# GpSimd takes over the high-word scaling of the weight conversions and half of the early softmax normalisation

## The chip, the cores and the metric

The kernel runs on one core of a Trainium2 chip. The metric is the device time of one execution in microseconds. TensorE (PE), VectorE (DVE), ScalarE (ACT) and GpSimd (POOL) each work through their own queue of instructions in order; SyncE (SP) issues the DMA transfers.

## The reference

A causal attention over a window of 128 positions, with a linear bias by distance for each of 8 heads, feeds two MLPs. Cut to what matters:

```python
scores = (q @ k.T) / 8 + bias          # 4 batches, 8 heads, 576 positions, head size 64
scores = where(0 <= i - j < 128, scores, -1e9)
attn = exp(scores - max);  attn = attn / (sum(attn) + 1e-9)
x = (attn @ v)                         # as 2304 tokens x 512
x = (s * relu(x @ w_in1)**2 + b) @ w_out1     # 512 -> 2048 -> 512
out = relu(x @ w_in2)**2 @ w_out2             # the same shape
```

All inputs and the output are float32. The four weight matrices reach the chip as 64-bit words: the host hands in float64 copies, viewed as integers.

## The kernel before, in words

**Weights.** Each weight matrix comes in four groups of 512 rows or columns of the hidden size. A load on SP's queue fills a tile `st...` of 128 partitions with 1024 or 512 pairs of 32-bit words (the low word and the high word of a float64). `convert` turns such a tile into float32 and splits it into a rounded part (`wih`, `woh`) and the rest (`wil`, `wol`), so that products of rounded parts in three passes stand for a float32 product. Its chain of seven steps goes from engine to engine: L123 on ACT (low word), L124 on DVE (sign), L125 (high word times 2^-112, in place; this is the line of the change), L126 on DVE (a shift, in place), L127 on POOL (integer add of the two words), L99 on ACT (rounded copy), L105 on DVE (the rest). Words of a kind lie 8 bytes apart in the tile. There are 14 conversions of 1024 words a partition and 4 of 512 for the first MLP, which all lie in the first 160 us, and 32 of 512 for the second, which lie between 508 and 658 us.

**Attention.** `pair_unit` handles 256 (or 128 + 256) query rows of two heads. Its first half makes scores on PE (L249), adds the bias tile `bases` on DVE (L190), takes exponentials on ACT (L194) and reciprocals of the sums on DVE (L197, L198). Its second half divides (L270 for the first head of the units of batch 0, L272 for all else), transposes the probabilities on PE (L274), copies the transposes out of PSUM on ACT (L99), multiplies with v on PE (L285) and splits the result into `x0h`, `x0l` (ACT, then DVE L102). In the names, `f_0_2woh` is the probability tile of batch 0's row block 0, units 2 and 3, `nd_0_3` the sums of unit 3, `t_0_3` its transposes, `u_0_3` its output. The eight units of batch 0 (u = 0 and 1, four pairs of heads) are the early ones. They come first in the program, together with the conversions of group 0 (`st_211`, `st_265`, `st_315`, `st_326`) and the first of group 1 (`st_337`, `st_480`).

**MLPs.** `mlp` runs over the hidden size in steps of 128: L361 (first product, 12 matmuls), ACT L371, DVE L372, ACT L99, DVE L105, then L398 or L407 (second product). Attention units and conversions are interleaved as pieces "behind" these steps, and a scheduler then sets each engine's order.

**Bias tiles.** The eight `bases` (L79) are made on POOL before anything else there, one for each head:

```python
nc.gpsimd.tensor_scalar(bases[:, h, :], base, 8.0 * 2.0 ** (-8.0 * (h + 1) / H), None, ALU.mult)
```

Of the kernel before, what the change touches and what calls it, by code (L numbers as in the profile page):

```python
# [8 lines left out]
F32 = mybir.dt.float32  # L9
# [3 lines left out]
AF = mybir.ActivationFunctionType  # L13
ALU = mybir.AluOpType
# [5 lines left out]
def attention_mlp2_kernel(ctx, tc, first0, first1, qkv0, qkv1, qkvt, w_in1, w_out1, s_in, b_in, w_in2, w_out2, out):  # L20
# [7 lines left out]
    nc = tc.nc  # L28
    B, H = qkv0.shape[:2]
# [31 lines left out]
    base = ap.tile([P, 2 * W], F32, tag="pr", name="base", bufs=NPR)  # L61
# [14 lines left out]

    bases = ap.tile([P, H, 2 * W], mybir.dt.bfloat16, tag="bases", name="bases", bufs=1)
    for h in range(H):
        nc.gpsimd.tensor_scalar(bases[:, h, :], base, 8.0 * 2.0 ** (-8.0 * (h + 1) / H), None, ALU.mult)  # L79

    tqs = [ap.tile([P, 2, TAIL], F32, tag=f"tq{i}", name=f"tq{i}", bufs=1) for i in range(2)]
    for t in tqs:
# [8 lines left out]
    def split(hi, lo, src, copy, sub):  # L91
        copy(hi, src)
        sub(lo, src, hi.bitcast(F32))
# [4 lines left out]
    def act_copy(o, i):  # L98
        return nc.scalar.activation(o, i, AF.Copy)  # L99
# [13 lines left out]
    def convert(words, hi, lo):  # L113

        l32, h32 = words[..., 0], words[..., 1]
        with tc.issue_after(marks[-4]) if len(marks) > 3 else nullcontext():
            nc.scalar.activation(l32, l32.bitcast(U32), AF.Copy, scale=2.0 ** -29)  # L123
        nc.vector.scalar_tensor_tensor(l32, h32, -2 ** 31, l32, ALU.bitwise_and, ALU.bitwise_or)  # L124
        nc.scalar.activation(h32.bitcast(F32), h32.bitcast(F32), AF.Copy, scale=2.0 ** -112)  # L125
        nc.vector.tensor_scalar(h32, h32, 3, None, ALU.logical_shift_left)  # L126
        nc.gpsimd.tensor_tensor(l32, h32, l32, ALU.add)  # L127
        split(hi, lo, l32.bitcast(F32), act_copy, dve_sub)
# [5 lines left out]
    def group_loads(g, wts, w_in, w_out, staging, steps):  # L134
# [22 lines left out]
        def conv(i):  # L157
            _, k, n, step = parts[i]
            if k not in wts[g]:
                for j in (k, k + 1):  # L160
                    wts[g][j] = wp.tile([P, GF, DM], F32R, tag=f"{GTAGS[j]}{g}", name=f"{GTAGS[j]}{g}")
            hi, lo = wts[g][k], wts[g][k + 1]
            part = (slice(None), slice(n, n + step)) if k else (slice(None), slice(None), slice(n * P, (n + step) * P))
            convert(places.pop(i).rearrange("p a (n w) -> p a n w", w=2), hi[part], lo[part])
# [37 lines left out]
    def pair_unit(b, u, hp):  # L202
# [56 lines left out]
        def outputs():  # L259
            raw, den, probs, pts = (made[x] for x in ("raw", "den", "probs", "pts"))  # L260
            vr = raw[:, BLK + nj * P:n].rearrange("p (j a d) -> p j a d" if early else "p (a j d) -> p j a d", j=nj, d=D)
            for i, (_, ncol) in enumerate(tiles):
                tp = (psum("h", f"t{nm}").rearrange("p (i n) -> p i n", n=P) if early and not (i or u) else
                      ps.tile([P, 4, P], F32, tag="t", name=f"t{nm}{i}", bufs=1))
                m = 0
                for a in range(2):
                    pr = probs[a][:, i, :ncol]
                    rden = den[:, 2 * a + i:2 * a + i + 1]
                    if early and a == 0:
                        nc.scalar.activation(pr, pr, AF.Copy, scale=rden)  # L270
                    else:
                        nc.vector.tensor_scalar(pr, pr, rden, None, ALU.mult)  # L272
                    for j in range(ncol // P):
                        nc.tensor.transpose(tp[:, m, :], pr[:, j * P:(j + 1) * P], ident)  # L274
                        m += 1
                moved = act_copy(pts[i][:, :m, :], tp[:, :m, :])
            up = ps.tile([P, 3 * P], F32, tag="u", name=f"u{nm}", bufs=1) if hp % 2 or u or not early else psum("o", f"u{nm}")

            with tc.issue_after(moved.ins):
                k = 0  # L280
                for i, (ka, ncol) in enumerate(tiles):
                    nk = ncol // P
                    for j in range(nk):
                        for a in range(2):
                            nc.tensor.matmul(up[a * D:(a + 1) * D, i * P:(i + 1) * P], vr[:, ka // P + j, a, :],  # L285
                                             pts[i][:, a * nk + j, :], start=(k == 0), stop=(j == nk - 1),
                                             skip_group_check=True)
                        k += 1
            xh, xl = xt[(b, u)]
            split(xh[:, hp, :], xl[:, hp, :], up[:, :BLK], act_copy if early and u else act_mark, dve_mark)  # L290
# [153 lines left out]
    def psum(tag, name):  # L444
        return pools["ps"].tile([P, DM], F32, tag=tag, name=name)
# [184 lines left out]
```

## Time and profile before

| what | value |
|---|---|
| time, median of 3 runs | 999.97 us (999.9 to 1000.04) |
| span of the profiled execution, first to last instruction | 996.9 us |
| left between that span and the median | 3.1 us |
| busy: PE, DVE, ACT, POOL | 968.4, 519.4, 489.5, 80.6 us |
| mean granted TensorE clock | 0.983 of full speed |

The page gives the profiled execution's span and no other time of it; 3.1 us of the median lie around it. Busy time is an average over stages: the first 160 us (attention of batch 0 and the conversions of the first MLP) look unlike the rest, so they are read by themselves.

### The profile page before, as it was taken

The page shows a single profiled execution, that of the slowest core. Times are in us where ns is not written, and L with a number is a line of the kernel's source. Part 1 is how long each engine was busy: PE and PEld are TensorE (multiplying, and loading weights), DVE is VectorE, ACT ScalarE, POOL GpSimd, SP SyncE. Part 2 cuts the span into 40 slices and gives each one's busy share as a digit, 9 for nine tenths or more (in the row PEclk, how much of TensorE's full clock was granted, in tenths as well). Part 3 has the DMA queues.
Part 4 walks back from the last instruction along what each step waited for, and adds up shares of the span by engine and source line. Part 5 has one row for each costly group of instructions (what it writes and reads, how often), then busy time and mean ns, then how long its engine had stood idle before and what let it go on. Part 6 is the DMA issues. An engine that isn't in the chain of part 4 may idle for free.

```text
span 996.9 us, 16799 instructions
## 1 busy us (share of the span) xinstructions
PE 968.4 (97%) x6504; PEld 852.6 (86%) x6504; DVE 519.4 (52%) x1268; ACT 489.5 (49%) x1157; POOL 80.6 (8%) x86
## 2 busy tenths in 40 slices
PE   7999899999999999999999999999999999999997
PEld 4699689999999999999999888778888888898886
DVE  6986886344764647646266787744222322422222
ACT  7976766455565545644255677654222321322121
POOL 4320320000000000000011222210000000000000
PEclk9699989999999999999999999999999999999999
DMA  8144423111221212211052445422000100100001
GB/s 337 44 157 152 149 94 107 54 54 34 67 65 42 78 29 74 75 46 29 27 178 85 131 170 155 137 75 84 1 1 22 43 1 1 43 1 22 1 1 42
DMA packets 46927, 72.39 MB, mean 73 GB/s; under 512 B 6656, under 2 KB 27136, under 8 KB 46848
## 3 DMA queue, kind: packets, MB, share of 16 engines
q1 hardware_dynamic: 46848, 71.32, 22.0%
q8 instruction: 51, 0.84, 0.4%
q14 instruction: 28, 0.23, 0.1%
HBM read 59.77 MB, written 11.53 MB: 72 GB/s over the span
## 4 chain that ended last, share of the span: by engine, by line
PE 77%; DMA 8%; ACT 6%; DVE 6%; issue 2%; POOL 0%; SPq 0%; ACTq 0%; DVEq 0%; POOLq 0%
PE ob L407 15%; PE hb L361 14%; PE ha L361 14%; PE oa L398 13%; DMA st<-w_out 4%; PE oc L398 3%; PE s L249 3%; PE u L285 3%; PE hc L361 3%; DMA st<-w_in 3%; PE t L274 2%; PE hbtail L361 2%; PE obtail L407 2%; DMA xib<-acc 1%; DVE wil L105 1%
## 5 line engine op out<-in xcount | busy, mean ns | idle before, releaser
L398 PE MATMUL oa<-ga,woh 128*128 128x256 f32 x960 | 188.7, 288 | 4.4 <-DVE ga L105 2.3
L407 PE MATMUL ob<-woh,gb 128*128 128x512 f32 x512 | 168.7, 390 | 1.2 <-ACT gb L99 1.2
L398 PEld LDWEIGHTS oa<-ga,woh 128*128 128x128 f32 x960 | 151.6, 191 | 9.0 <-DVE ga L105 3.1
L398 PE MATMUL oa<-ga,wol 128*128 128x256 f32 x480 | 135.9, 286 | 0.0
L372 DVE SCALAR_TENSOR_TENSOR rb<-hb,rb 128x512 f32<-128x512 f32 x64 | 44.1, 690 | 147.4 <-ACT rb L371 147.2
L407 PEld LDWEIGHTS ob<-woh,gb 128*128 128x128 f32 x512 | 96.0, 188 | 23.1 <-ACT gb L99 3.2
L371 ACT ACTIVATE rb<-hb 128x512 f32<-128x512 f32 x64 | 38.2, 596 | 156.3 <-PE hb L361 152.0
L407 PE MATMUL ob<-wol,gb 128*128 128x512 f32 x256 | 99.7, 389 | 0.0
L398 PEld LDWEIGHTS oa<-ga,wol 128*128 128x128 f32 x480 | 91.7, 191 | 1.3 <-issue 0.9
L127 POOL TENSOR_TENSOR st<-st 128x512 int32<-128x512 int32 (+1 forms) x50 | 68.9, 1379 | 285.1 <-DVE st L126 285.1
L372 DVE SCALAR_TENSOR_TENSOR ra<-ha,ra 128x256 f32<-128x256 f32 x120 | 50.1, 418 | 49.0 <-ACT ra L371 48.1
L105 DVE TENSOR_TENSOR ga<-ra,ga 128x256 fp32r<-128x256 f32 x120 | 57.1, 478 | 26.6 <-ACT ga L99 25.9
L105 DVE TENSOR_TENSOR gb<-rb,gb 128x512 fp32r<-128x512 f32 x64 | 45.5, 710 | 44.0 <-ACT gb L99 43.9
L99 ACT ACTIVATE ga<-ra 128x256 fp32r<-128x256 f32 x120 | 49.2, 413 | 38.0 <-DVE ra L372 36.0
L371 ACT ACTIVATE ra<-ha 128x256 f32<-128x256 f32 x120 | 45.1, 377 | 42.6 <-PE ha L361 41.3
L99 ACT ACTIVATE gb<-rb 128x512 fp32r<-128x512 f32 x64 | 40.4, 631 | 47.6 <-DVE rb L372 35.6
L124 DVE SCALAR_TENSOR_TENSOR st<-st 128x512 int32<-128x512 int32 (+1 forms) x50 | 46.7, 937 | 25.1 <-ACT st L123 24.7
L123 ACT ACTIVATE st<-st 128x512 int32<-128x512 uint32 (+1 forms) x50 | 40.9, 822 | 33.0 <-DMA st<-w_out 19.9
L407 PEld LDWEIGHTS ob<-wol,gb 128*128 128x128 f32 x256 | 48.1, 188 | 9.8
L194 ACT ACTIVATE pr<-pr,nd 128x256 f32<-128x256 f32 (+1 forms) x96 | 45.1, 472 | 6.3 <-DVE nd L190 6.3
L190 DVE CUSTOM_DVE_ANT_0 pr<-s,bases 128x256 f32<-128x256 f32 (+1 forms) x96 | 31.9, 386 | 23.7 <-PE t L274 14.6
L125 ACT ACTIVATE st<-st 128x512 f32<-128x512 f32 (+1 forms) x50 | 40.7, 818 | 5.7 <-DVE st L124 5.7
(204 smaller groups left out, 2348.6 us busy)
## 6 DMA issues: line engine op xcount, KB each, us to landing
st<-w_out SPq DMA_DIRECT2D x20, 512.0 KB, 3.9
st<-w_in SPq DMA_DIRECT2D x8, 1024.0 KB, 6.0
st<-w_in SPq DMA_DIRECT2D x16, 512.0 KB, 4.5
st<-w_out SPq DMA_DIRECT2D x6, 1024.0 KB, 9.8
raw<-qkv SPq DMA_DIRECT2D x36, 128.0 KB, 2.6
xib<-acc SPq DMA_DIRECT2D x9, 512.0 KB, 4.6
out<-obb SPq DMA_DIRECT2D x16, 256.0 KB, 2.0
raw<-qkv SPq DMA_DIRECT2D x24, 160.0 KB, 3.0
```

What stands on the lines that cost most here:

```text
L99: return nc.scalar.activation(o, i, AF.Copy)
L105: nc.vector.tensor_tensor(o, a, b_, ALU.subtract)
L123: nc.scalar.activation(l32, l32.bitcast(U32), AF.Copy, scale=2.0 ** -29)
L124: nc.vector.scalar_tensor_tensor(l32, h32, -2 ** 31, l32, ALU.bitwise_and, ALU.bitwise_or)
L125: nc.scalar.activation(h32.bitcast(F32), h32.bitcast(F32), AF.Copy, scale=2.0 ** -112)
L127: nc.gpsimd.tensor_tensor(l32, h32, l32, ALU.add)
L194: nc.scalar.activation(pr, pr, AF.Exp, bias=nmx, scale=-1.0, accum_out=den)
L361: nc.tensor.matmul(ph, w_[:, cc, j * P:(j + 1) * P], x_[:, cc, :], start=(k == 0), stop=(k == 3 * NCC - 1))
L371: nc.scalar.activation(r, ph, AF.Relu)
L372: nc.vector.scalar_tensor_tensor(r, ph, 0.0, r, ALU.max, ALU.mult)
L398: nc.tensor.matmul(po[o // 2][:, (o % 2) * BLK:(o % 2 + 1) * BLK], w_[:, j, o * P:(o + 1) * P], g[:, gi, :], start=(start and n == 0 and o ...
L407: nc.tensor.matmul(po[t], g[:, gi, t * P:(t + 1) * P], w_[:, j, :], start=(start and n == 0), stop=(stop and n == 2))
```

## The change

Three operations are written for POOL as a tensor_scalar with two multiplications, the second by 1.0. L79 was on POOL already, with one multiplication. L125 (50 instructions: 14 on 1024 words, 36 on 512) and L270 (16 instructions: 12 on 128x256, 4 on 128x128) were on ACT.

```diff
     for h in range(H):
-        nc.gpsimd.tensor_scalar(bases[:, h, :], base, 8.0 * 2.0 ** (-8.0 * (h + 1) / H), None, ALU.mult)
+        nc.gpsimd.tensor_scalar(bases[:, h, :], base, 8.0 * 2.0 ** (-8.0 * (h + 1) / H), 1.0, ALU.mult, ALU.mult)
...
         nc.vector.scalar_tensor_tensor(l32, h32, -2 ** 31, l32, ALU.bitwise_and, ALU.bitwise_or)
-        nc.scalar.activation(h32.bitcast(F32), h32.bitcast(F32), AF.Copy, scale=2.0 ** -112)
+        nc.gpsimd.tensor_scalar(h32.bitcast(F32), h32.bitcast(F32), 2.0 ** -112, 1.0, ALU.mult, ALU.mult)
         nc.vector.tensor_scalar(h32, h32, 3, None, ALU.logical_shift_left)
...
                     if early and a == 0:
-                        nc.scalar.activation(pr, pr, AF.Copy, scale=rden)
+                        nc.gpsimd.tensor_scalar(pr, pr, rden, 1.0, ALU.mult, ALU.mult)
                     else:
                         nc.vector.tensor_scalar(pr, pr, rden, None, ALU.mult)
```

The scheduler orders every queue anew. On ACT, early in the program (units 0 and 1 of batch 0 and the first conversion, `st_211`), the difference reads so:

```order
 L123 ACTIVATE st_211<-st_211 128x1024
 L194 ACTIVATE f_0_0wih,nd_0_1_171<-f_0_0wih,nd_0_1_171 128x128
-L270 ACTIVATE f_0_0wih<-f_0_0wih,nd_0_0_128 128x128
-L270 ACTIVATE f_0_0wih<-f_0_0wih,nd_0_0_128 128x256
 L194 ACTIVATE f_0_0wih,nd_0_1_171<-f_0_0wih,nd_0_1_171 128x256
-L125 ACTIVATE st_211<-st_211 128x1024
 L194 ACTIVATE f_0_0wih,nd_0_1_171<-f_0_0wih,nd_0_1_171 128x128
```

Here the exponentials of unit 1 follow each other with nothing of L270 or L125 between them.

On POOL, a little later (units 2 and 3, the other three conversions of group 0), the queue that held the L127 alone now reads so:

```order
+L270 TENSOR_SCALAR f_0_2woh<-f_0_2woh,nd_0_2_214 128x256
+L125 TENSOR_SCALAR st_265<-st_265 128x1024
+L125 TENSOR_SCALAR st_315<-st_315 128x1024
+L125 TENSOR_SCALAR st_326<-st_326 128x1024
 L127 TENSOR_TENSOR st_265<-st_265 128x1024
 L127 TENSOR_TENSOR st_315<-st_315 128x1024
+L270 TENSOR_SCALAR f_0_2woh<-f_0_2woh,nd_0_3_268 128x128
+L270 TENSOR_SCALAR f_0_2woh<-f_0_2woh,nd_0_3_268 128x256
 L127 TENSOR_TENSOR st_326<-st_326 128x1024
```

The division of unit 3's first head stands behind three L125 and two L127.

On PE, where that division is waited for (`t_0_3_285`, the first transposes of unit 3), two score products of unit 1_1 and four products of unit 2 moved ahead of it:

```order
 L249 MATMUL s_1_10_437<-raw_1_1_434 128x256 x2
+L249 MATMUL s_1_11_438<-raw_1_1_434 128x256 x2
+L285 MATMUL u_0_2_247<-f_0_2wol,rwil 64x128 x4
 L274 MATMUL t_0_3_285<-ident,f_0_2woh 128x128 x2
 L361 MATMUL ha_0_348<-x0h,wih_256 128x256
```

The first products of the MLP (`ha_0`) stand behind those transposes in both orders.

## Rows read from the trace of the kernel before

**Rows 1.** The page, parts 1 and 4: busy time, chain by engine.
```profile
PE 968.4 (97%) x6504; PEld 852.6 (86%) x6504; DVE 519.4 (52%) x1268; ACT 489.5 (49%) x1157; POOL 80.6 (8%) x86
...
PE 77%; DMA 8%; ACT 6%; DVE 6%; issue 2%; POOL 0%; SPq 0%; ACTq 0%; DVEq 0%; POOLq 0%
```
**Rows 2.** Windows: length, busy us of PE, PEld, DVE, ACT, POOL, clock, DMA, GB/s.
```profile
15.00:20.00 5.00, 4.82 (x21) 3.11 (x21) 4.38 (x20) 4.96 (x16) 0.00 (x0) 1.00 1.02 419
20.00:25.00 5.00, 3.18 (x24) 2.04 (x22) 4.50 (x14) 5.00 (x11) 0.00 (x0) 1.00 0.71 232
25.00:30.00 5.00, 5.00 (x23) 3.21 (x17) 4.54 (x7) 5.00 (x14) 2.01 (x2) 0.51 0.02 5
...
35.00:40.00 5.00, 5.00 (x28) 3.75 (x24) 4.93 (x11) 5.00 (x11) 0.43 (x1) 0.62 0.24 45
...
540.00:657.00 117.00, 112.94 (x673) 99.01 (x673) 88.53 (x146) 80.15 (x154) 30.52 (x29) 1.00 0.46 147
```
**Rows 3.** Timeline of PE, 0 to 56 us: start, length, instruction, idle before.
```profile
22.99 0.44 PE L285 MATMUL u<-f_0wil,rwih 128*64 128x128 f32 x4 [0.67 <-ACT f_0wil L99]
24.58 0.66 PE L285 MATMUL u<-f_0wil,rwih 128*64 128x128 f32 x8 [1.15 <-ACT f_0wil L99]
...
28.84 0.69 PE L274 MATMUL t<-ident,f_2woh 128*128 128x128 f32 x2
...
30.10 2.07 PE L249 MATMUL s<-raw 64*128 64x256 f32 x4
...
34.61 1.12 PE L285 MATMUL u<-f_2wol,rwil 128*64 128x128 f32 x8
```
**Rows 4.** Timeline of ACT, 0 to 56 us.
```profile
9.46 0.78 ACT L270 ACTIVATE f_0wih<-f_0wih,nd 128x128 f32<-128x128 f32 x2
...
10.92 1.15 ACT L125 ACTIVATE st<-st 128x1024 f32<-128x1024 f32 x1 [0.19 <-DVE st L124]
...
23.85 0.68 ACT L99 ACTIVATE f_0wil<-t 128x512 f32<-128x512 f32 x1
...
24.58 0.90 ACT L270 ACTIVATE f_2woh<-f_2woh,nd 128x128 f32<-128x128 f32 x2
```
**Rows 5.** Groups of ACT by line: count, busy us, mean ns, idle before.
```profile
L125 ACT ACTIVATE st<-st 128x512 f32<-128x512 f32 (+1 forms) x50 | 40.7, 818 | 5.7 <-DVE st L124 5.7
...
L270 ACT ACTIVATE f_0wih<-f_0wih,nd 128x256 f32<-128x256 f32 x6 | 3.0, 561 | 0.0
```
**Rows 6.** Timeline of POOL.
```profile
2.88 0.40 POOL L65 TENSOR_SCALAR_AFFINE_SELECT base<-base 128x256 f32<-128x256 f32 x1
9.41 0.85 POOL L79 TENSOR_SCALAR bases<-base 128x256 bf16<-128x256 f32 x1
12.88 1.89 POOL L127 TENSOR_TENSOR st<-st 128x1024 int32<-128x1024 int32 x1 [2.62 <-DVE st L126]
...
540.03 1.04 POOL L127 TENSOR_TENSOR st<-st 128x512 int32<-128x512 int32 x1 [26.24 <-DVE st L126]
```
**Rows 7.** Timeline of DVE, single instructions of the first 23 us.
```profile
8.97 0.44 DVE L272 TENSOR_SCALAR f_0wih<-f_0wih,nd 128x128 f32<-128x128 f32 x1
9.46 1.42 DVE L124 SCALAR_TENSOR_TENSOR st<-st 128x1024 int32<-128x1024 int32 x1
12.97 1.82 DVE L197 TENSOR_SCALAR nd<-nd 128x4 f32<-128x4 f32 x1 [0.18 <-ACT f_0wih L194]
16.85 0.17 DVE L197 TENSOR_SCALAR nd<-nd 128x4 f32<-128x4 f32 x1
21.61 1.23 DVE L124 SCALAR_TENSOR_TENSOR st<-st 128x1024 int32<-128x1024 int32 x1 [0.15 <-ACT st L123]
```
**Rows 8.** Tiles `wih` and `woh`, 560 to 680 us: duration min/median/max, first and last start.
```profile
L361 PE MATMUL hb<-y0h,wih x64: 388/389/498, 587.3 to 678.1; 128*128 128x512 f32 x64
...
L105 DVE TENSOR_TENSOR wol<-st,woh x12: 675/684/693, 584.7 to 660.0; 128x512 fp32r<-128x512 f32 x12
```

## The prediction

> **What bounds the kernel now.** First the page: PE is busy 97% of the span and makes 77% of the chain that ended last; ACT and DVE make 6% each [rows 1]. For most of the run it therefore does not matter what ACT does, and the change can act only where PE waits or runs slowly. The windows show where that is. From 15 to 40 us ACT is busy 4.96 to 5.00 us of every 5, DVE 4.38 to 4.93, and PE, though shown busy, gets half its clock from 25 us on (0.51 in the slice 25 to 30, level 1.2 GHz), after a slice in which it was busy only 3.18 us of 5 [rows 2]. PE's timeline shows what it stood for there: two waits of 0.67 and 1.15 us, both for ACT's copy of transposes [rows 3]. After 160 us PE is back to back until the weights of the second MLP come, 540 to 657 us, where it is busy 112.9 of 117 us, ACT 80.2 and DVE 88.5 [rows 2]. So three stages can move: the first 50 us, the rest of the first 160, and 540 to 657.
>
> **What leaves ACT.** L125 was 50 instructions and 40.7 us, L270 sixteen of about 0.5 us (six of them 0.561 us each on average) [rows 5]; some 48 us of ACT's 490. The part that can be worth something lies ahead of the two waits of PE. There ACT ran one L125 (1.15 us) and three pairs of L270 (0.78 us for the first, the other two alike) [rows 4], 3.5 us in all, while it had no idle time from 15 us on. The copies that PE waited for come that much earlier at most, so both waits (1.8 us) can go: **-1.8**. The L270 of unit 3 (0.90 us at 24.58) stood behind them and is met again below.
>
> **The clock.** If PE has no hole between 22 and 25 us, its slice looks like that of 15 to 20, in which it was busy 4.82 of 5 us and held 1.00 [rows 2], and the fall at 25 us may not come. The rows show the half level from 25 to beyond 35 us (0.62 over 35 to 40, so three quarters of that slice). At full clock 13.7 us of work would take 6.8. PE would then wait for DVE instead, which is busy 4.50, 4.54 and 4.93 us in these slices: about 0.3 us free in each 5, some 2 us over 15 to 45. I take what DVE leaves: **-2**.
>
> **What a POOL instruction costs.** No row shows the new form: two multiplications, float32 in and out. Below it is bounded by the affine_select (one float32 input and output, 128x256, 0.40 us), above by L79 itself (one multiplication, bfloat16 out, 0.85 us) [rows 6]. L127's two shapes give a fixed part of 2 x 1.04 - 1.89 = 0.19 us. So 1024 words take (0.40 - 0.19) x 4 + 0.19 = 1.03 us at the low end, 2.83 at the high end by the same working, and 3.40 if L79's time is all per element. L127 stands between, with 1.89 us for 1024 and 1.04 for 512 words, and is the nearest row: it runs on the same tile, with words 8 bytes apart, 32 bits in and out. I take it: 1.89, 1.04, and for L270 0.61 (256) and 0.40 (128).
>
> The Trainium skill, GPSIMD Engine Reference, section Engine selection, calls GpSimd's one-input operations roughly line-rate, and its section Specifications gives 1.2 GHz; that would be an estimated 0.85 us for 1024 words and no POOL term in the sum. L79's row, 0.85 us for 256, does not agree; the affine_select comes nearer.
>
> **POOL's queue.** POOL was idle while ACT did this work, so most of the added 50 + 16 instructions is free. The exception is the division of unit 3. On ACT it ran at 24.58 [rows 4]; PE used it at 28.84 [rows 3]. Now it stands behind three L125 and two L127. The first of these L125 can start when L124 has ended, 21.61 + 1.23 = 22.84 [rows 7], and the 128x128 part of L270 is done at 22.84 + 3 x 1.89 + 2 x 1.89 + 0.40 = 32.7. PE comes to these transposes later than before by what was put ahead of them, 2.07 + 1.12 us at the half clock [rows 3]: 28.84 + 3.2 = 32.0. PE, with `ha_0` queued behind, waits **+0.7**. At 1.03 us it is 30.0, no wait; at 3.40 it is 37.3 (with 0.52 for the L270), a wait of 5.3. The wait begins at 1.66 us for an L125.
>
> **DVE beside POOL.** L197 at 12.97 took 1.82 us where it takes 0.17: it ended with the L127 of 12.88 to 14.77, so that a tensor_scalar on DVE waits for POOL's instruction [rows 6, 7]. Against L79 the same holds for L272, 0.44 us at 8.97, ending as the L79 of 9.41 starts. But L124, which has two inputs, started at 9.46 beside that L79 and took 1.42 against 1.23 us: 0.2 us, not the 0.8 that were left. So a one-input POOL instruction seems to hold back L126, L272 and L197, and L124 or L105 hardly. L126 needs its own L125 anyway, and in the new order most of DVE's other work fills the time. I take **0**, with the other reading as a rival.
>
> **L79** in the new form starts at the same time; the scores need one tile at a time and found theirs. **0**.
>
> **Rest of the first 160 us.** ACT loses about 1.15 us in each conversion, POOL gains 1.89; I take **0**. **540 to 657 us:** 28 L125 of 1.04 us are 29 us more for POOL, which has 30.5 of 117 [rows 2]. The last `wol` is ready at 660.7, and PE still runs first products with the last `wih` at 678 [rows 8], with second products behind them: some 15 us of slack cover a later chain, **0**; without that cover each 512-word conversion would be late by the 1.04 less ACT's 0.67.
>
> **Sum.** -1.8 - 2 + 0.7 = -3.1 us, on a span of 996.9: 993.8, and with the 3.1 us around it 996.9. The profiled execution plus those 3.1 us is the median by construction, so I forecast 997, or 994 to 998 for this case (the clock term from 0 to -2, the wait of 0.7 gone at the low price, one further us of ACT's waits gone).
>
> **Rivals.**
> *POOL is as slow as L79* (2.8 to 3.4 us for 1024 words, 1.5 to 1.7 for 512). For it: the only tensor_scalar on POOL in the trace. Against it: the affine_select. Then unit 3's wait is 5.3 us, a little less at 2.8, and in 540 to 657 us POOL gains 45 us. DVE's own 88.5 less some 13 for PSUM inputs, POOL's 30.5 and these 45 come to 151 of 117, 34 too much if they exclude each other; less the 15 of slack that is up to +19. Together 1005 to 1025, 1018 as its middle. It decides from about 1.66 us upward. Chance 0.24.
> *The shared port.* POOL's instruction holds back every DVE instruction with two SBUF inputs, L124 and L105 too. For it: L197's 1.82 us; against it: L124's 1.42 [rows 7]. In 10 to 50 us DVE's instructions of these kinds take about 25 us and POOL's 12; six L125 (11.3) and some twelve L270 (6.7) make it 55 of 40, 15 too much. ACT's relief hides some: 1003 to 1013. Chance 0.18.
> The Trainium skill, SBUF — State Buffer, section Who interferes with whom, says that either engine blocks for the whole instruction, two-input instructions included. By that rule this rival is the forecast; the L124 beside L79 does not agree.
> *The clock holds and PE uses it*: all of 6.8 us, with the waits gone too, 991 to 993. Against it: DVE's slices. Chance 0.12.
> *No difference*: the copies PE waits for are late for another reason, and the two 1.8 us come back as waits for DVE: 998 to 1002. Chance 0.16.
>
> **Chances.** What a measurement can tell is 0.2%, 2 us. The forecast has 0.30, and with the held clock faster comes to 0.42; same 0.16; slower 0.24 + 0.18 = 0.42. As both signs hold much, the range takes in the held clock and most of the slow POOL: 989 to 1028. The forecast's own range is 994 to 998.
>
> **What would show it.** Right: an L125 of 1024 words near 1.9 us or less on POOL, no ACT wait of PE between 22 and 25 us, a granted clock above 0.51 from 25 to 35 us, `t_0_3` at PE within 1 us of 32, PE busy as before from 540 to 657. Wrong: POOL rows near 3 us, DVE rows of L126, L105 or L272 stretched by the POOL instruction beside them, a PE hole before the first `ha`, or idle PE with `gb` late on DVE after 587 us.

## The result, and the profile after

The changed kernel takes **1011.92 us** (median of 4 runs, 1009.46 to 1015.06) against 1000.0 for the kernel before in the same session: ratio 1.0117, 95% interval 1.0102 to 1.0132. It is slower by about 12 us. The forecast was 997, the range 989 to 1028. The profiled execution, the fastest of the four (1009.46), has a span of 1007.7 us, 10.8 more than before. Some 1.8 us lie around that span, not the 3.1 that the prediction added. The rows below have to explain those 10.8.

The page, parts 1 and 4 (beside [rows 1]):

```profile
PE 969.9 (96%) x6504; PEld 852.6 (85%) x6504; DVE 538.3 (53%) x1268; ACT 449.9 (45%) x1091; POOL 141.5 (14%) x152
...
PE 77%; DVE 11%; DMA 6%; ACT 4%; issue 2%; POOL 1%; SPq 0%; ACTq 0%; DVEq 0%; POOLq 0%
```

ACT lost 39.6 us of busy time, where the prediction took some 48 us off it. But DVE, with the same 1268 instructions, is busy 18.9 us longer, and its share of the chain went from 6% to 11% while ACT's fell.

Where the time went is read from two tiles that each appear once in the program: `pc` (the end of the first MLP) and `hbtail` (near the end of the second). For before and then after, the first and last start:

```profile
L549 PE MATMUL pc<-ones,csum x8: 250/250/271, 495.2 to 496.0; 128*128 128x1 f32 x8
...
L361 PEld LDWEIGHTS hbtail<-ytailh,wih x64: 187/192/192, 852.6 to 898.8; 128*128 128x128 f32 x64
```

```profile
L549 PE MATMUL pc<-ones,csum x8: 250/250/271, 502.0 to 502.8; 128*128 128x1 f32 x8
...
L361 PEld LDWEIGHTS hbtail<-ytailh,wih x64: 187/192/192, 863.4 to 909.6; 128*128 128x128 f32 x64
```

Up to `pc` the changed kernel loses 502.0 - 495.2 = 6.8 us; from there to `hbtail` it takes 361.4 us against 357.4 and loses 4.0 more; behind that nothing. The first loss is called the *first stage* below, the second the *second stage*. Each covers the conversions of one MLP.

The windows (beside [rows 2]):

```profile
20.00:25.00 5.00, 4.29 (x24) 2.41 (x22) 4.97 (x8) 3.88 (x13) 3.38 (x2) 1.00 0.67 229
25.00:30.00 5.00, 2.61 (x14) 1.77 (x12) 5.00 (x9) 1.36 (x5) 5.00 (x4) 0.89 0.02 3
...
35.00:40.00 5.00, 4.03 (x22) 3.40 (x21) 4.92 (x11) 2.82 (x6) 3.06 (x3) 0.58 0.09 17
...
540.00:657.00 117.00, 110.70 (x683) 98.02 (x682) 97.06 (x148) 62.91 (x123) 54.54 (x54) 0.99 0.45 147
```

From 25 to 30 us PE falls from 5.00 to 2.61 us of work, ACT from 5.00 to 1.36, and DVE and POOL are both busy all 5 us. In the second stage DVE grows from 88.5 to 97.1.

PE's timeline in that place (beside [rows 3]) shows what it waits for now:

```profile
21.26 0.70 PE L285 MATMUL u<-f_0wil,rwih 128*64 128x128 f32 x4 [0.71 <-ACT f_0wil L99]
...
28.61 1.81 PE L249 MATMUL s<-raw 64*128 64x256 f32 x4 [2.39 <-DVE nd L190]
32.93 2.07 PE L249 MATMUL s<-raw 64*128 64x256 f32 x4 [2.52 <-DVE nd L190]
...
35.99 0.69 PE L274 MATMUL t<-ident,f_2woh 128*128 128x128 f32 x2
```

Two waits of 2.39 and 2.52 us for DVE stand where there were waits of 0.67 and 1.15 for ACT; of those, one of 0.71 is left. What DVE did ahead of the two L190 (beside [rows 7]):

```profile
20.32 4.40 DVE L124 SCALAR_TENSOR_TENSOR st<-st 128x1024 int32<-128x1024 int32 x3
24.64 1.60 DVE L126 TENSOR_SCALAR st<-st 128x1024 int32<-128x1024 int32 x1
26.16 1.05 DVE L197 TENSOR_SCALAR nd<-nd 128x4 f32<-128x4 f32 x1
...
28.47 1.63 DVE L126 TENSOR_SCALAR st<-st 128x1024 int32<-128x1024 int32 x1
30.02 2.17 DVE L272 TENSOR_SCALAR f_2woh<-f_2woh,nd 128x128 f32<-128x128 f32 x2
```

and POOL in the same microseconds (beside [rows 6]):

```profile
21.62 5.56 POOL L125 TENSOR_SCALAR st<-st 128x1024 f32<-128x1024 f32 x3 [3.46 <-DVE st L124]
27.16 4.69 POOL L127 TENSOR_TENSOR st<-st 128x1024 int32<-128x1024 int32 x2
31.84 0.97 POOL L270 TENSOR_SCALAR f_2woh<-f_2woh,nd 128x128 f32<-128x128 f32 x2
```

The reader can do the sum. With the engine to itself DVE takes 1.25 us for an L124 of 1024 words, 0.72 for an L126 and at most 0.38 for a division (measured in the first experiment below), and 0.17 for L197 [rows 7]. So the first group is 4.40 - 3 x 1.25 = 0.65, 1.60 - 0.72 = 0.88 and 1.05 - 0.17 = 0.88 too long, 2.4 us in all, before a PE wait of 2.39. The second group is 0.91 and 1.41 too long, 2.3 us, before a wait of 2.52. POOL too is stretched: the same L125 takes 1.15 us alone, and three of them take 5.56. The new order has a part in the first wait as well: in the kernel before, the four L190 of 23.89 to 25.27 us stood right behind two L124, and now the first two of them stand behind three L124, two L126 and an L197. The sum does not tell holds and places in the queue apart.

The longest new wait of PE comes later, for a division on DVE. PE, then DVE and POOL ahead of it, and last the same four divisions in the kernel before:

```profile
123.17 0.66 PE L274 MATMUL t<-ident,pr 128*128 128x128 f32 x2 [3.91 <-DVE pr L272]
...
115.92 1.11 DVE L197 TENSOR_SCALAR nd<-nd 128x4 f32<-128x4 f32 x1
...
117.77 2.29 DVE L126 TENSOR_SCALAR st<-st 128x1024 int32<-128x1024 int32 x1
...
121.12 2.63 DVE L272 TENSOR_SCALAR pr<-pr,nd 128x128 f32<-128x128 f32 x4
...
116.96 2.55 POOL L127 TENSOR_TENSOR st<-st 128x1024 int32<-128x1024 int32 x1
120.14 2.80 POOL L127 TENSOR_TENSOR st<-st 128x1024 int32<-128x1024 int32 x1 [0.63 <-DVE st L126]
```

```profile
112.28 1.01 DVE L272 TENSOR_SCALAR pr<-pr,nd 128x128 f32<-128x128 f32 x4
```

Here 0.94, 1.57 and 1.62 us, 4.1 in all, are holds before a wait of 3.91, and two of the three lie beside additions (L127), which were on POOL before the change too. In the first 160 us PE's waits add up to 21.9 us, against 15.9 before: 6.0 of the 6.8 us of the first stage.

The groups of POOL give the prices:

```profile
L125 POOL TENSOR_SCALAR st<-st 128x512 f32<-128x512 f32 x36 | 27.2, 755 | 136.8 <-DVE st L124 82.0 <-DMA st<-w_in 54.8
L125 POOL TENSOR_SCALAR st<-st 128x1024 f32<-128x1024 f32 x14 | 19.8, 1423 | 60.7 <-DMA raw<-qkv 27.8 <-DVE st L124 16.6 <-DVE nd L197 11.5
...
L79 POOL TENSOR_SCALAR bases<-base 128x256 bf16<-128x256 f32 x8 | 3.1, 403 | 0.3
```

L125 costs 1.42 us for 1024 words and 0.76 for 512, less than the 1.89 and 1.04 of the forecast. POOL is faster than forecast, and the kernel is slower all the same.

### The profile page after: what moved, and what is told of

It is laid out like the page before. It is cut to its first block, busy times and chain, and to the rows that moved or that the text cites. A ratio compares the mean times of both kernels' runs of the same rounds, so it can differ in the third digit from the quotient of the medians.

```text
span 1007.7 us, 16809 instructions
## 1 busy us (share of the span) xinstructions
PE 969.9 (96%) x6504; PEld 852.6 (85%) x6504; DVE 538.3 (53%) x1268; ACT 449.9 (45%) x1091; POOL 141.5 (14%) x152
## 4 chain that ended last, share of the span: by engine, by line
PE 77%; DVE 11%; DMA 6%; ACT 4%; issue 2%; POOL 1%; SPq 0%; ACTq 0%; DVEq 0%; POOLq 0%
PE ob L407 15%; PE hb L361 14%; PE ha L361 14%; PE oa L398 13%; DMA st<-w_out 3%; PE oc L398 3%; PE hc L361 3%; PE u L285 3%; PE s L249 3%; PE hbtail L361 2%; PE obtail L407 2%; DVE st L124 2%; PE t L274 2%; DMA st<-w_in 2%; DVE st L126 1%
## 5 line engine op out<-in xcount | busy, mean ns | idle before, releaser
L127 POOL TENSOR_TENSOR st<-st 128x512 int32<-128x512 int32 (+1 forms) x50 | 76.6, 1532 | 35.9 <-DVE st L126 30.8
L125 POOL TENSOR_SCALAR st<-st 128x512 f32<-128x512 f32 (+1 forms) x50 | 47.0, 942 | 197.5 <-DVE st L124 98.6
L105 DVE TENSOR_TENSOR gb<-rb,gb 128x512 fp32r<-128x512 f32 x64 | 47.2, 738 | 45.5 <-ACT gb L99 45.2
L105 DVE TENSOR_TENSOR ga<-ra,ga 128x256 fp32r<-128x256 f32 x120 | 56.0, 469 | 25.8 <-ACT ga L99 25.5
L124 DVE SCALAR_TENSOR_TENSOR st<-st 128x512 int32<-128x512 int32 (+1 forms) x50 | 52.4, 1052 | 24.8 <-ACT st L123 24.7
L190 DVE CUSTOM_DVE_ANT_0 pr<-s,bases 128x256 f32<-128x256 f32 (+1 forms) x96 | 31.9, 386 | 24.0 <-PE t L274 14.6
```

The lines of the kernel that those rows point to most:

```text
L105: nc.vector.tensor_tensor(o, a, b_, ALU.subtract)
L125: nc.gpsimd.tensor_scalar(h32.bitcast(F32), h32.bitcast(F32), 2.0 ** -112, 1.0, ALU.mult, ALU.mult)
```

## The experiments

**Theories.** *Port*: an instruction of POOL keeps DVE's instructions on SBUF waiting (and the other way round), so that work given to POOL is paid for by DVE, on which PE waits. *Queue*: divisions and conversions wait longer in POOL's own queue. *Order*: the scheduler set every queue anew, and the new order happens to be worse. The table gives every run of the whole kernel; times are medians, ratios are to the kernel before on the same chip with 95% intervals, and the two stages are those of the profiled execution, worked out from `pc` and `hbtail` as above (before: 495.2 and 357.4). One execution can lie several us from its median (the profiles of e12 and e15 are of the slowest of their runs, 1009.1 and 1005.1), so a stage's number is good to a few us and the two do not always add up to the median's difference.

| run | time us | ratio | first stage | second stage |
|---|---|---|---|---|
| changed kernel | 1011.92 | 1.0117 (1.0102 to 1.0132) | +6.8 | +4.0 |
| e1 divisions only | 1009.75 | 1.0092 (1.0065 to 1.0120) | +7.0 | +1.3 |
| e2 L125 of the first MLP only | 1009.04 | 1.0089 (1.0071 to 1.0107) | +7.3 | +2.0 |
| e3 L125 of the second MLP only | 1003.34 | 1.0021 (1.0005 to 1.0036) | +1.7 | +4.7 |
| e4 extra work, two multiplications | 1006.95 | 1.0068 (1.0042 to 1.0095) | +4.4 | +4.8 |
| e6 bias tiles only | 999.39 | 0.9985 (0.9973 to 0.9998) | +0.1 | +0.1 |
| e7 moved work left out | 1000.15 | 0.9992 (0.9980 to 1.0004) | -6.1 | +7.3 |
| e8 divisions on DVE | 1002.50 | 1.0016 (1.0001 to 1.0030) | +1.6 | +2.2 |
| e10 before, no additions | 1001.03 | 1.0006 (0.9990 to 1.0023) | +4.4 | -1.4 |
| e11 changed, no additions | 1000.41 | 1.0015 (0.9991 to 1.0038) | -2.9 | +2.9 |
| e12 changed, L125 with one multiplication | 1005.64 | 1.0052 (1.0032 to 1.0072) | +7.6 | +2.8 |
| e13 extra work, one multiplication | 993.77 | 0.9929 (0.9909 to 0.9948) | -0.9 | -4.9 |
| e14 extra work, one word each | 1003.11 | 1.0029 (1.0016 to 1.0042) | +1.8 | +2.4 |
| e15 divisions only, one multiplication | 1002.11 | 1.0008 (0.9991 to 1.0025) | +5.1 | +1.3 |
| e16 changed, with one-word extras | 1007.21 | 1.0069 (1.0052 to 1.0085) | +8.8 | 0.0 |
| e17 more extra work, two | 1012.92 | 1.0127 (1.0108 to 1.0146) | +8.2 | +5.6 |
| e18 more extra work, one | 995.48 | 0.9961 (0.9941 to 0.9981) | +0.3 | -4.1 |

**The engines by themselves (e5, e9).** The kernel's body is replaced by stages of four instructions:

```diff
+    for p_ in (pool_two, pool_one, pool_add):     # GpSimd alone
+        stage(None, p_)
+    for d in (dve_sign, dve_shift, dve_sub, dve_div):
+        stage(d, None)
+    for p_ in (pool_two, pool_add):               # both at once
+        for d in (dve_sign, dve_shift, dve_sub, dve_div):
+            stage(d, p_)
```

> The kernel's work is left out wholly; what runs is sixteen-odd stages of four instructions each, of 128x1024 words (divisions 128x256), on GpSimd alone, VectorE alone, and both at once. If the two share a port that one holds for a whole instruction, an instruction that takes a us alone beside one that takes b us shows up to a+b: the two-multiplication scaling on GpSimd (1.13 us alone) beside the sign insertion (1.23 alone) gives about 2.3 us per pair instead of the longer of the two, and so for the shift (0.69), the subtraction (about 1.2) and the division. If the engines only share memory bandwidth a little, each pair takes at most 1.3 times the longer alone. If the excluding pairs are only some, the table says which. One-multiplication scaling: about 3.4 us from the 851 ns for 128x256 of the bias tiles, against 1.1 to 1.6 for two.

Timelines of DVE and POOL (the lines are those of this small kernel: L43 is the sign insertion as L124, L46 the shift as L126, L55 the scaling with two multiplications, L58 with one, L61 the addition as L127; four instructions in a row but for the 16 of L55):

```profile
30.20 7.57 DVE L43 SCALAR_TENSOR_TENSOR st<-st 128x1024 int32<-128x1024 int32 x4 [22.65 <-ACT st L66]
37.80 5.95 DVE L46 TENSOR_SCALAR st<-st 128x1024 int32<-128x1024 int32 x4
...
58.12 5.01 DVE L43 SCALAR_TENSOR_TENSOR st<-st 128x1024 int32<-128x1024 int32 x4 [1.27 <-ACT st L66]
63.17 2.88 DVE L46 TENSOR_SCALAR st<-st 128x1024 int32<-128x1024 int32 x4
...
72.63 1.52 DVE L52 TENSOR_SCALAR pq<-pq,den 128x256 f32<-128x256 f32 x4 [1.54 <-ACT pq L66]
75.42 9.72 DVE L43 SCALAR_TENSOR_TENSOR st<-st 128x1024 int32<-128x1024 int32 x4 [1.27 <-ACT st L66]
...
5.21 4.62 POOL L55 TENSOR_SCALAR su<-su 128x1024 f32<-128x1024 f32 x4 [4.79 <-DVE su L32]
9.92 11.67 POOL L58 TENSOR_SCALAR su<-su 128x1024 f32<-128x1024 f32 x4
21.67 7.80 POOL L61 TENSOR_TENSOR su<-su 128x1024 int32<-128x1024 int32 x4
29.55 26.77 POOL L55 TENSOR_SCALAR su<-su 128x1024 f32<-128x1024 f32 x16
```

DVE runs alone from 58 to 74 us: 1.25 us for a sign insertion, 0.72 for a shift. Beside the scaling (30 to 44 us) they take 1.89 and 1.49, beside the addition (from 75 us) the sign insertion takes 2.43. And the scaling itself goes from 4.62 / 4 = 1.15 us to 26.77 / 16 = 1.67. With two SBUF inputs or one, DVE's instruction is held. The hold is not whole: a sign insertion beside the scalings takes 1.89 us, about midway between the 1.25 of two engines that do not meet and the 1.25 + 1.15 = 2.40 of two that take turns for the whole instruction. That is less than the 2.3 expected for turns and more than the 1.6 (1.3 times the longer) expected for a shared bandwidth. The scaling with one multiplication takes 11.67 / 4 = 2.92 us, two and a half times as long as with two.

> The kernel's work is left out wholly; stages of four instructions on VectorE and on GpSimd as in the first such run, which showed the two alternating, each pair of a 1.15 us scaling and a 1.25 us sign insertion taking 2.02 us. Here: the one-multiplication scaling (2.85 us alone) beside the sign insertion and the subtraction; if it is not held apart, both run at their own time (1.25 on VectorE), and if it is, VectorE's mean is near 3 to 4 us. The bias tile in either form beside the sign insertion: before's trace had 1.42 against 1.23, so at most 1.5 in the one-multiplication form; in the other form more, about 1.6. A memset on GpSimd: no expectation between held and not. VectorE's subtraction and copy that read PSUM beside the add: if only memory read by both matters they are held too, since they write SBUF; the row of the scores in the changed kernel (379 against 383 ns) says not held. VectorE's four-word instruction beside adds: held to about 1.9 each.

In e9 L46 is the sign insertion, L58 a subtraction that reads PSUM and SBUF, L64 the four-word instruction as L197, L70 the scaling with one multiplication, L82 the addition:

```profile
8.79 2.87 DVE L58 TENSOR_TENSOR rr<-pp,hh 128x512 f32<-128x512 f32 x4 [0.64 <-ACT hh L89]
...
17.53 0.78 DVE L64 TENSOR_SCALAR pq<-pq 128x4 f32<-128x4 f32 x4 [1.54 <-ACT pq L87]
23.70 6.05 DVE L46 SCALAR_TENSOR_TENSOR st<-st 128x1024 int32<-128x1024 int32 x4 [5.39 <-ACT st L87]
...
74.32 2.87 DVE L58 TENSOR_TENSOR rr<-pp,hh 128x512 f32<-128x512 f32 x4 [13.58 <-ACT hh L89]
...
91.71 4.03 DVE L64 TENSOR_SCALAR pq<-pq 128x4 f32<-128x4 f32 x4 [5.97 <-ACT pq L87]
...
23.05 40.40 POOL L70 TENSOR_SCALAR su<-su 128x1024 f32<-128x1024 f32 x12
...
74.16 7.80 POOL L82 TENSOR_TENSOR su<-su 128x1024 int32<-128x1024 int32 x4 [0.95 <-ACT su L87]
```

Beside the scaling with one multiplication the sign insertion takes 1.51 us, not 3 to 4: this form hardly holds DVE, though POOL is busy with it without a break (and is itself slowed, to 40.40 / 12 = 3.37 us). The subtraction that reads PSUM takes 2.87 us alone and 2.87 beside the addition: not held at all. The four-word instruction takes 0.20 us alone and 1.01 beside additions, where 1.9 was expected. In this run the GpSimd work of one stage ran on into the next, so the bias tile's two forms and the memset were not measured beside DVE.

**Parts of the change (e1, e2, e3, e6).** Each is the kernel before with one part; in e2 and e3 the scaling goes to POOL for one MLP alone.

```diff
 # e1
-                        nc.scalar.activation(pr, pr, AF.Copy, scale=rden)
+                        nc.gpsimd.tensor_scalar(pr, pr, rden, 1.0, ALU.mult, ALU.mult)
 # e2 ("bp" not in pools) and e3 ("bp" in pools): L125
+        if "bp" not in pools:
+            nc.gpsimd.tensor_scalar(h32.bitcast(F32), h32.bitcast(F32), 2.0 ** -112, 1.0, ALU.mult, ALU.mult)
+        else:
             nc.scalar.activation(h32.bitcast(F32), h32.bitcast(F32), AF.Copy, scale=2.0 ** -112)
 # e6: L79
-        ..., None, ALU.mult)
+        ..., 1.0, ALU.mult, ALU.mult)
```

> Only the 16 divisions (L270) go to GpSimd; L125 and L79 stay as before. Port theory (each added GpSimd instruction holds VectorE up through a shared port, and VectorE is full in the first 50 us): some 6 us of added GpSimd time there, a third to a half of it lost on TensorE, 1001 to 1003 us. Queue theory (the loss comes from the new order of the queues, above all from unit 3's division behind three L125 and two L127): without L125 on GpSimd it stands behind nothing, 999 to 1000.5 us. Relief theory (my prediction): 998 to 1000 us.

> Only the L125 of the 18 conversions of the first MLP go to GpSimd. Port theory: 14 x 1.13 + 4 x 0.66 us = 18 us more GpSimd time in the first 160 us; of the changed kernel's 7.2 us lost by 180 us this part should hold 4 to 7: 1004 to 1007 us. Queue theory: the three L125 still stand ahead of two L127, but no division is behind them: 1000 to 1003 us. After 180 us no difference by either.

> Only the L125 of the 32 conversions of the second MLP go to GpSimd. Port theory: 32 x 0.66 us = 21 us more GpSimd time between 508 and 660 us, VectorE instructions there stretched as in the changed kernel, TensorE waits for ga and gb: 1003 to 1005 us. Queue theory: no division and no attention there, and 15 us of slack before the weights are needed: 1000 to 1001 us.

> Only the bias tiles take two multiplications; nothing else moves. They come from 851 to about 400 ns each, done some 3.6 us earlier, at a time when VectorE waits for loads. All theories: within 1 us of before (999 to 1001.5); a gain over 1 us would say that the sign insertion beside them, 1.42 us against 1.23, was held by them and on the path.

The bias tiles are worth nothing (-0.15%, within a measurement's reach of none); e6 is the only one of these runs whose four queues keep the order of the kernel before, so this is the form alone. The other three each lose, e1 more than any theory had expected of it (1003 us at most), e2 more than the port's 1004 to 1007, e3 within the port's range. They do not lose in sum: 8.8 + 8.0 + 2.3 is 19 us where the whole change loses 12. By stages they fit better: the second stage loses 4.7 us with e3 and 4.0 with the whole, the first loses 7.0 with e1, 7.3 with e2 and 6.8 with both. Either part alone is enough for the first stage's loss, and the two together cost no more; a sum of independent costs cannot explain that. Nor does the sum of the holds give the time: in e1 DVE is busy 522.6 us, 3.2 more than before, and the kernel loses 8.8.

**Was ACT the bound? (e7, e8).** e7 leaves L125 and the first head's divisions out altogether (a mask in L126 keeps the words finite), e8 puts those divisions on DVE.

```diff
 # e7
-        nc.scalar.activation(h32.bitcast(F32), h32.bitcast(F32), AF.Copy, scale=2.0 ** -112)
-        nc.vector.tensor_scalar(h32, h32, 3, None, ALU.logical_shift_left)
+        nc.vector.tensor_scalar(h32, h32, 3, 0x3fffffff, ALU.logical_shift_left, ALU.bitwise_and)
 # e7, and in e8 without the condition
-                    if early and a == 0:
-                        nc.scalar.activation(pr, pr, AF.Copy, scale=rden)
-                    else:
+                    if not (early and a == 0):
                         nc.vector.tensor_scalar(pr, pr, rden, None, ALU.mult)
```

> The scaling of the high words and the normalisation of the first head of each early unit are left out altogether (so values are not scaled and that head not normalised); the shift gets a mask as second operation, so that the words stay finite. ScalarE is relieved by all that the change takes from it, and GpSimd gets nothing. If ScalarE bounded the early stages, the time falls by 4 to 8 us (992 to 996): then the change's idea is good and what it loses is GpSimd's doing, 16 to 20 us of it. If VectorE and not ScalarE is what TensorE waits for, as the trace of the changed kernel says, it falls by under 2 us (998 to 1000), and the loss of about 12 is all GpSimd's.

> The eight pairs of divisions go to VectorE instead of GpSimd: ScalarE is relieved of 8 us, VectorE gets 16 more instructions of 0.35 to 0.6 us, 5 to 8 us in the first 60 us, GpSimd nothing. If VectorE bounds the first 60 us, most of this shows: 1003 to 1007. If ScalarE bounds there, the time falls to 996 to 999. If neither, 999 to 1001.

e7 as a whole is no faster, which by its expectation would say that ACT bounds nothing. The stages say otherwise: 6.1 us gained by `pc`, 7.3 lost in the second stage. Its waits from 480 to 700 us:

```profile
PE ob L408 <- ACT gb L99: 3.8, 2, 3.1
PE ha L362 <- DVE ra L373: 1.7, 1, 1.7
```

No work was added there, though POOL is busy 33.4 us from 540 to 657 against 30.5 with the same additions, and the granted clock is 0.97 against 1.00. The queues stand in another order; that this makes the loss is likely and not shown. The relief of the first stage was real (part of it is that one head's division is off the path). e8 is 2.2 us slower with the divisions on DVE (between the ranges for "DVE bounds" and "neither"), where e1 is 8.8 with the same divisions on POOL: the "idle" engine was the dearer place.

**Port or queue: without the additions (e10, e11).** L127 is left out of the kernel before and of the changed kernel (so the weights lack their upper words).

```diff
-        nc.gpsimd.tensor_tensor(l32, h32, l32, ALU.add)
```

> The kernel before with the integer addition on GpSimd left out (so the weights lack their upper words), 50 instructions of 69 us. It is the base of the next run. If what GpSimd holds of VectorE costs time already in the kernel before, it is faster by 3 to 8 us (992 to 997); if the addition cost only by its place in the chain of a conversion, by 0 to 2.

> The changed kernel with the same addition left out. GpSimd then has nothing that the moved instructions queue behind but one another. If they cost by queueing behind additions and delaying them, it is within 2 us of the run without additions on the kernel before. If they cost by holding VectorE, the 64 us of scalings and divisions still hold it, and it is slower than that run by 4 to 10 us.

Both are within 0.2% of before. e10 gains nothing, though DVE is busy 27.2 us less (492.2 against 519.4): in the kernel before the additions' holds are hidden. Without additions the change costs nothing either (1000.4 against 1001.0). By the expectations on record that speaks for the queue, and the port's 4 to 10 us did not come; but POOL is then busy 66 us and not 141, less than in the kernel before, so the port has no more to hold there than before's additions, which cost nothing. The expectation of the port was drawn too simply and the pair does not decide. DVE's busy time is 8.6 us longer in e11 than in e10 (500.8 and 492.2), so holds are there, and they cost nothing. In these orders the moved work costs only on top of the additions, which fits the wait of 3.91 us behind two additions above.

**Port or queue: work that nobody waits for (e4, e13, e17, e18, e14).** Two or three instructions of 256 words after each addition of the kernel before (four or two in e17 and e18), into a tile that nobody reads. The form is the difference: two multiplications hold DVE, one multiplication takes POOL longer and hardly holds it.

```diff
         nc.gpsimd.tensor_tensor(l32, h32, l32, ALU.add)
+        for _ in range(3 if prod(l32.shape[1:]) > DM else 2):      # e17, e18: 4 and 2
+            nc.gpsimd.tensor_scalar(scr..., l32..., 1.0, 1.0, ALU.mult, ALU.mult)    # e4, e17
+            nc.gpsimd.tensor_scalar(scr..., l32..., 1.0, None, ALU.mult)             # e13, e18
+            nc.gpsimd.tensor_scalar(scr[:, :1], l32[:, 0, :1]..., 1.0, 1.0, ALU.mult, ALU.mult)   # e14
```

> The kernel before, with nothing moved: behind each L127 two (512 words) or three (1024 words) more tensor_scalar instructions of 256 words run on GpSimd, whose result nobody reads. They add about the GpSimd time that L125 took in the changed kernel (some 1.2 and 0.8 us a conversion, 45 us in all) and give ScalarE nothing. Port theory: VectorE is held up as in the changed kernel, without the relief: 1006 to 1014 us. Queue theory: nothing of the attention waits for GpSimd, the queues of the other engines are nearly those of before: 999.5 to 1002 us.

> The kernel before with the extra instructions that nobody reads, two or three after each addition, in the one-multiplication form: some 0.85 us each instead of 0.65 as held, so GpSimd is busy 25 us longer than with the other form (which gave 1006.95), and holds VectorE little. Port: 999 to 1003. Queue: 1006 to 1012.

> The kernel before with the same number of extra instructions, of one word each (about 0.1 us). Neither queue nor port: 999 to 1002 by both. What it shows beyond that is what the order of the instructions and the later release of the staging tiles are worth by themselves; 1004 or more would mean that the order explains most of the run with extra instructions of 256 words.

> The kernel before with extra instructions of 256 words in the two-multiplication form, four after each addition of 1024 words and two after each of 512. Port: 1003 to 1010, as in the first such run (1006.95). If order decides: anything from 994 to 1007.

> The same in the one-multiplication form. Port: 4 us or more faster than its twin in the two-multiplication form, since VectorE is held less. Queue: slower than its twin by 2 to 6 us, as GpSimd is busy longer. If order decides, the difference can have either sign and the first pair's 13 us does not come again.

Part 1 of the page, e4 and then e13:

```profile
PE 970.7 (96%) x6504; PEld 852.2 (85%) x6504; DVE 530.6 (53%) x1268; ACT 488.8 (49%) x1157; POOL 156.8 (16%) x200
```

```profile
PE 963.2 (97%) x6504; PEld 848.8 (86%) x6504; DVE 530.1 (53%) x1268; ACT 487.6 (49%) x1157; POOL 209.5 (21%) x200
```

POOL is 53 us busier in e13, and the kernel is 13 us faster. The second pair repeats it: 1012.9 and 995.5, 17 us. That is the opposite of what a longer queue on POOL would do, so this queue is out as the cause. The order is not out. The traces show that the scheduler set the queues anew with the form: of DVE's 1268 instructions 165 stand elsewhere in e13 than in e4, and 167 in e18 than in e17. Between e4 and e17 it is 47, between e13 and e18 it is 36, so the second pair repeats the first one's orders along with its forms and is no independent test. The window 600 to 660 us of e17 and then e18 shows where:

```profile
600.00:660.00 60.00, 55.22 (x251) 45.03 (x249) 44.81 (x67) 36.29 (x64) 34.46 (x42) 0.97 0.41 126
```

```profile
600.00:660.00 60.00, 59.58 (x259) 47.81 (x258) 42.41 (x64) 38.32 (x65) 48.03 (x44) 1.00 0.45 133
```

PE loses 4.8 of 60 us beside the two-multiplication form and 0.4 beside the other, with POOL at 34 and 48 us. Two things stay open. DVE's busy time over the whole run is the same in e4 and e13, so it is not the sum of the holds that counts, and which holds fell on PE's path was not traced beyond the window above. And e13 and e18 are faster than the kernel before by 6.7 and 4.9 us, more than its median varies, though they only add work. Their order may have to do with it; no run shows why they beat both kernels. e14 was to show what another order is worth, and is 2.7 us slower where at most 2 were expected. But its one-word instructions took 0.38 us each and not 0.1, 43.6 us of POOL in all, so it does not measure the order alone.

**The changed kernel in other forms and orders (e12, e15, e16).**

```diff
 # e12: L125 of the changed kernel; e15: e1 in the same way
-        nc.gpsimd.tensor_scalar(h32.bitcast(F32), h32.bitcast(F32), 2.0 ** -112, 1.0, ALU.mult, ALU.mult)
+        nc.gpsimd.tensor_scalar(h32.bitcast(F32), h32.bitcast(F32), 2.0 ** -112, None, ALU.mult)
 # e16: the changed kernel with the one-word instructions of e14
```

> The changed kernel, with the scaling of the high words in the one-multiplication form. Beside VectorE that form took GpSimd 3.37 us for 1024 words instead of 1.15 alone, and VectorE's sign insertion took 1.51 us beside it instead of 1.25 (1.9 to 2.0 beside the other form). GpSimd is busy some 60 us longer, and holds VectorE less. Port: VectorE's busy time falls from 538 to about 525 and the time from 1012 to 1001 to 1008. Queue: each conversion's addition and each early division waits up to 2.2 us longer, and the time rises to 1013 to 1025.

> The kernel before with only the divisions moved to GpSimd, in the one-multiplication form: 0.85 us for 256 words by the bias tiles instead of 0.4 to 0.64, sixteen of them, 7 us more on the path of the early units by price alone. The two-multiplication form gave 1009.75. Port: shorter holds of VectorE, 1003 to 1008. Queue and price: 1010 to 1015.

> The changed kernel with two or three one-word instructions on GpSimd after each addition (about 0.1 us each), which let the scheduler come to another order. If the 12 us are what the changed work costs, 1007 to 1016. If they are mostly the order that the change happened to get, as far as the same instructions moved the kernel before (2.7 us) and further: 999 to 1006.

With L125 in the slow form that hardly holds DVE the change loses 5.2 us and not 11.9, though POOL is busy 193.5 us and not 141.5; the divisions alone lose 1.7 and not 8.8. Both go the port's way and against the queue's ranges, and e15 is the pair closest in order: 69 of DVE's instructions stand elsewhere than in e1, 230 in e12 than in the changed kernel. But DVE's busy time in e12 fell only to 535.1 us, where 525 was expected, so here too the sum of the holds does not tell the time, and the first stages of the profiled executions show little or nothing of the gain (+7.6 for e12 against +6.8, +5.1 for e15 against +7.0). e16 is the same work in one other order, with one-word instructions on top, and loses 6.8.

## Why the prediction was wrong

**The step that failed** is "DVE beside POOL ... I take 0". Its larger half is a price: the prediction granted that an instruction of POOL holds L126, L197 and L272, and put this at nothing because other work would fill DVE's time. DVE had no such room: it was busy all 5 us from 25 to 30. Of the 2.4 us of holds before the first of PE's waits, 1.76 are of L126 and L197; the 2.3 before the second and the 4.1 before the third are all of these three lines. The smaller half is that L124 and L105 went free, on one row: the L124 that took 1.42 us beside an L79 and not the 2 it would have needed [rows 7]. But that L79 had one multiplication. e5 and e9 show that this form hardly holds the sign insertion (1.51 us), while the form that the change brings, and the additions that were there all along, do (1.89 and 2.43 against 1.25). The row was read rightly and carried over to an instruction that behaves otherwise. The trace of the kernel before had a row that says so of the additions, an L124 beside the L127 of 33.54 to 35.43 us, twice as long as alone:

```profile
34.06 2.45 DVE L124 SCALAR_TENSOR_TENSOR st<-st 128x1024 int32<-128x1024 int32 x1
```

**What follows from it on the path.** The forecast let DVE have 0.3 us free in each 5 from 15 to 45 us and gave the early stage to ACT's two waits. With DVE nearly full, 2.4 and 2.3 us of holds in 20 to 32 us came out as PE's waits of 2.39 and 2.52, and 4.1 us at 116 to 123 us as one of 3.91. The first stage ended 6.8 us late, where -3.1 was forecast.

**What leaves ACT (-1.8)** had its sign right: ACT is busy 1.36 of 5 us where it was full, one of the two waits is gone (0.71 is left of the other), and with POOL out of it (e7) the first stage gains 6.1. **The clock (-2):** it held longer, 0.89 against 0.51 from 25 to 30 us, but PE was at work only 2.61 us of that slice, and over 35 to 40 us the clock was 0.58. e12's clock stayed at 1.00 up to 50 us with a first stage 7.6 us late. As the prediction said, DVE bounds what a held clock can bring; the bound was nothing and not 2.

**The price on POOL** was mis-sized the other way: 1.89 us taken for 1024 words, 1.15 alone and 1.42 on average. The upper bound came from L79, whose own time fell from 0.85 to 0.40 us with the second multiplication; the affine_select's 1.03 was the nearest. **POOL's queue (+0.7):** unit 3's division ran from 31.84 to 32.81, close to the 32.7 worked out for its first part, by luck: the first L125 started 1.2 us earlier than forecast, and three of them took 1.85 us each, near the 1.89 of the sum, beside a busy DVE, where one alone takes 1.15. PE came to the division at 35.99, held up by DVE, so no wait was left to pay.

**540 to 657 us (0)** failed too: the second stage lost 4.0 us. The 15 us of slack were those of the weights. What PE waits for there are `ga` and `gb`, the activations whose last step, L105, is on DVE between the steps of the conversions. PE's waits for that step from 480 to 700 us, for the kernel before and then for the changed one (us in total, times, the longest):

```profile
PE oa L398 <- DVE ga L105: 1.5, 3, 0.7
```

```profile
PE oa L398 <- DVE ga L105: 4.3, 4, 1.9
PE ob L407 <- DVE gb L105: 1.4, 3, 0.8
```

With its waits for ACT, which fell from 3.1 to 1.2 us, PE waited 2.3 us longer in the second stage. The granted clock makes up the rest by estimate: it was 0.92 from 605 to 610 us, where PE stood for the longest of these waits, and 0.74 from 610 to 615, where it was 1.00 before, 0.34 x 5 = 1.7 us of full clock. Slack of one product of an engine is not slack of the others in its queue. **L79 (0)** was right (e6).

**The rivals.** The shared port came nearest: 1003 to 1013 us at a chance of 0.18, with 1011.9 measured. Its wording, "two SBUF inputs", names a part only: one-input instructions are held as well (L126 from 0.72 to 1.49 us), as the prediction itself had granted and priced at 0. Slow POOL (0.24) is out by its price. How the 12 us divide between the holds and the order that this change happened to get stays open: e16 loses 6.8 us in another order, and no experiment that moved work to POOL or changed its form there, but for the bias tiles, kept the order fixed. The holds are measured; that they make the whole loss is not shown.

The Trainium skill, SBUF — State Buffer, section Who interferes with whom, holds that VectorE and GpSimd share a pair of ports for a whole instruction, VectorE instructions with one SBUF input outside its two-port modes excepted. The prediction named it and set it aside for the L124 row. The runs agree with it on the PSUM exception (2.87 us either way). They agree in direction for the two-multiplication scaling and the addition: the sign insertion took 1.89 and 2.43 us beside them, where turns of whole instructions would give 2.40 and 3.20 by the times alone. They do not agree for the scaling with one multiplication, 1.51 us where a whole instruction's wait would have given nearly 3.

## What to carry to other kernels

Work moved to an idle GpSimd was not free here, where VectorE had no room: ask what VectorE does in the same microseconds, and look for a small VectorE instruction that takes as long as the GpSimd instruction beside it. Take the evidence of a hold from the very form of instruction that the change brings, and measure the pair by itself if the trace lacks it. And compare stage by stage at fixed marks of the program: a kernel whose scheduler orders everything anew can move by several microseconds for reasons that its totals hide (e7: -6.1 and +7.3).

## What the hardware showed that was not expected

- On GpSimd a tensor_scalar with two multiplications is 2.5 times as fast as with one: 1.15 against 2.92 us for 1024 words, 0.40 against 0.85 for the 128x256 bias tile.
- The slow form hardly holds VectorE (1.51 against 1.25 us), the fast one and the integer addition do (1.89 and 2.43).
- A VectorE subtraction with one operand in PSUM is not held by GpSimd's addition (2.87 us for four, both ways); a four-word instruction on SBUF takes 0.8 us longer beside it.
- Extra work on GpSimd that nobody reads made the kernel 0.7% faster in one form and 0.7% slower in the other, and 0.4% faster and 1.3% slower in a second pair; the orders differed too.
- A tensor_scalar of one word on GpSimd took 0.38 us (e14).
